# A third buffer for the attention output rows and two order edges on VectorE, with the mask and the dummy operand moved into idle buffers

## The chip, the cores and the metric

The kernel runs on one core of one Trainium2 chip. Its time is the device time of one execution in microseconds (us). It is the span that the profile shows, first to last instruction, plus 1.8 us. The profile also gives the mean clock that TensorE was granted: 1.0 is full speed.

## The reference

```python
h  = x + attention(layernorm(x)) @ wo        # x: 2048 tokens x 1024, bf16
h2 = h + mlp(layernorm(h))                   # gated MLP, hidden width 3584

phi = lambda t: where(t > 0, t + 1, exp(t)) + 1e-6
kv  = einsum("bhsd,bhse->bhde", phi(k), v)   # 32 heads of 32, linear attention
num = einsum("bhqd,bhde->bhqe", phi(q), kv)
o   = num / (einsum("bhqd,bhd->bhq", phi(q), sum_s phi(k)) + 1e-6)
```

## The kernel before

Three stages follow one another. Up to about 122 us, K and V are made and summed into `kv`. From there to about 290 us, the rows of the attention output are made, one row for each tile of 128 tokens, and the MLP's first products are fitted in between. From 290 us on, the MLP alone keeps TensorE busy. The change acts on the first two stages. I number the rows in the order in which they are made, from 0.

One row passes through these steps. Note the tags: a tag is a set of buffers that its tiles use in turn.

```python
def nd():                                      # the row's products and its division
    o_sb = bwork.tile([P, D], BF16, tag="o_sb", name="o_sb")      # bufs=2 from the pool
    for c0, n in pieces:                       # three pieces
        ps = ndpool.tile([P, NW], FP32, tag="ab", name="nd")      # one of three shared PSUM banks
        ...                                    # matmuls nd <- pqT, kvz
        nc.scalar.activation(out=den, ..., func=ACT.Ln)           # reciprocal on ScalarE
        nc.scalar.activation(out=rd, ..., func=ACT.Exp, scale=-1.0)
        nc.vector.tensor_tensor(out=ov[:, c0:c0 + n], in0=ndv, in1=rd, op=ALU.mult)
def oT():                                      # transpose of the row, a DMA from the SP queue
    nc.sync.dma_start_transpose(out=st["oT"], in_=st["o"][:])
def wo_h(borrow):                              # projection (attn), 2 x 8 matmuls, residual, normalization
    for j in range(2):
        if borrow: ps = pspool.tile(..., tag="E", bufs=2, name="attn")    # rows 6 to 9
        else:      ps = abpool.tile(..., tag="ab", name="attn")           # the same three banks as nd
        for c in range(KC):
            nc.tensor.matmul(ps[:], lhsT=st["oT"][:, c, :], rhs=wo_sb[:, c, ...], ...)
        added[t, j] = nc.vector.scalar_tensor_tensor(...)         # residual sum, frees the bank
    ...                                        # hn: two passes of ScalarE over the row
def hn_T():                                    # transpose of the normalized row, a DMA
    nc.sync.dma_start_transpose(out=hnT[s][i][:, :, r:r + P], in_=st["hn"][:])
```

The sums for the weights of the fast (Strassen) products are made by VectorE. Those of the query weights:

```python
def sums():
    nc.vector.tensor_tensor(out=t1, in0=b12, in1=b11, op=ALU.subtract)
    nc.vector.tensor_tensor(out=t2, in0=b22, in1=t1, op=ALU.subtract)     # "second sum"
    nc.vector.tensor_tensor(out=t3, in0=b22, in1=b12, op=ALU.subtract)    # "third sum"
    nc.vector.tensor_tensor(out=t4, in0=b21, in1=t2, op=ALU.subtract)
```

A scheduler decides, when the program is built, in which order each engine gets its instructions. It works from the program's dependences and buffers. This order then stays fixed: an engine that has come to an instruction waits there until its inputs are ready. The order of a built program can be read without running it.

## Time and profile before

| | before |
|---|---|
| median of its first three runs | 737.68 us (737.57 to 738.51) |
| span of the profiled execution | 737.2 us (its time, 739.0 us, is above that median) |
| TensorE busy | 722.7 us, 98% |
| longest waits of TensorE after the start | 0.8, 0.5, 0.5, 0.5 us |

The prediction shows the page and the waits. A line of the waits reads: engine, tile and source line that waited, the engine, tile and line waited for, then total us, times, longest us. A line of the timeline reads: start us, duration us, engine, source line, operation, out<-in, shape, count, and in brackets the idle time ahead of it with what ended it. `SPq` is the queue from which the DMAs are issued; its row is the issuing, not the moving of the data.

### The profile page before, as it was taken

To read this page: it belongs to the slowest core of one execution; us is meant where nothing else is said; L and a number is where in the kernel's file an instruction comes from. 1 tells how busy PE (TensorE), PEld (TensorE's weight loads), DVE (VectorE), ACT (ScalarE), POOL (GpSimd) and SP (SyncE) were. 2 spreads that over 40 slices of the span, in tenths; PEclk is the share of its full clock that TensorE was granted. 3 is DMA by queue.
4 is the path that set the end of the run, shared out by engine and by line. 5 is a ranking of instruction groups with operands and counts; after the bars stand their busy time and mean duration, and the time that the engine had idled before them with its cause. 6 is when DMAs were issued, how large, how long until landed. Compare 5 with 4: busy or idle time off the path is not lost.

```text
span 737.2 us, 10549 instructions
## 1 busy us (share of the span) xinstructions
PE 722.7 (98%) x3967; PEld 381.8 (52%) x4020; DVE 556.0 (75%) x980; ACT 321.5 (44%) x580; POOL 20.7 (3%) x56
## 2 busy tenths in 40 slices
PE   8999999999989999999999999999999999999997
PEld 3444555444444444444444444444444458888667
DVE  6997644676789767688768787887786479996677
ACT  4776553778786655444344444443444120000000
POOL 0000000000000000000000000000000001100210
PEclk9999999999999999999999999999999999999999
DMA  9765002079977526175638358575483499978932
GB/s 315 169 145 157 0 1 95 21 168 230 215 166 166 135 73 208 43 207 135 196 106 243 114 188 270 182 219 193 162 280 120 137 392 343 305 253 283 257 44 58
DMA packets 143811, 128.88 MB, mean 175 GB/s; under 512 B 50960, under 2 KB 126096, under 8 KB 143760
## 3 DMA queue, kind: packets, MB, share of 16 engines
q1 hardware_dynamic: 136688, 123.30, 55.6%
q0 software_dynamic: 5312, 3.15, 3.4%
q10 hardware_dynamic: 1760, 1.77, 0.7%
q8 instruction: 31, 0.51, 0.3%
q14 instruction: 20, 0.16, 0.1%
HBM read 76.81 MB, written 39.85 MB: 158 GB/s over the span
## 4 chain that ended last, share of the span: by engine, by line
PE 85%; DVE 7%; DMA 4%; ACT 3%; issue 1%; SPq 0%; DVEq 0%; POOL 0%; ACTq 0%
PE accA L832 22%; PE accX L832 8%; PE accY L832 8%; PE accA L1167 8%; PE attn L557 6%; PE Aq L733 4%; PE Aq L314 3%; PE accA L993 3%; PE accX L1167 3%; PE Aq L454 3%; PE accY L1167 2%; PE Eq L314 2%; PE accY L993 2%; PE accX L993 2%; PE Eq L733 2%; DVE stats L272 1%
## 5 line engine op out<-in xcount | busy, mean ns | idle before, releaser
L842 ACT ACTIVATE gu<-gu 128x512 bf16<-128x512 bf16 x72 | 45.4, 630 | 131.3 <-DVE gu L841 131.3
L837 ACT COPY snap<-accA 128x1024 f32<-128x1024 f32 x72 | 72.5, 1008 | 36.5 <-PE accA L832 36.4
L832 PEld LDWEIGHTS <-tg 128*128 128x128 f16 x384 | 37.6, 98 | 45.3
L832 PEld LDWEIGHTS <-tu 128*128 128x128 f16 x384 | 37.6, 98 | 45.3
L557 PE MATMUL attn<-wo_mem,oT 128*128 128x512 bf16 x247 | 57.9, 379 | 2.6 <-DVE o_sb L534 1.3
L841 DVE TENSOR_TENSOR gu<-accY,snap 128x1024 bf16<-128x1024 f32 x36 | 43.9, 1219 | 10.0 <-ACT snap L837 10.0
L832 PE MATMUL accA<-hn,tg 128*128 128x512 f16 (+1 forms) x192 | 49.3, 379 | 0.0
L832 PE MATMUL accA<-hn,tu 128*128 128x512 f16 (+1 forms) x192 | 49.3, 379 | 0.0
L841 DVE TENSOR_TENSOR gu<-accX,snap 128x1024 bf16<-128x1024 f32 x36 | 43.9, 1219 | 6.4 <-PE accX L832 3.7
L154 ACT COPY u<-Aq 128x512 f32<-128x512 f32 x54 | 31.3, 581 | 36.6 <-PE Aq L314 19.3
L1167 PEld LDWEIGHTS <-x 128*128 128x128 f16 (+1 forms) x448 | 43.9, 98 | 5.5
L832 PEld LDWEIGHTS <-wu 128*128 128x128 bf16 x288 | 28.2, 98 | 34.0
L832 PEld LDWEIGHTS <-wg 128*128 128x128 bf16 x288 | 28.2, 98 | 34.0
L557 PEld LDWEIGHTS <-oT 128*128 128x128 bf16 x256 | 24.6, 98 | 32.5 <-issue 4.1
L845 DVE TENSOR_TENSOR hq<-gu 128x512 bf16<-128x512 bf16 x48 | 20.3, 423 | 14.3 <-ACT gu L842 14.2
L314 PEld LDWEIGHTS <-xT 128*128 128x128 bf16 (+1 forms) x192 | 18.6, 98 | 23.6 <-issue 2.3
L534 DVE TENSOR_TENSOR o_sb<-nd,rd 128x384 bf16<-128x384 f32 (+1 forms) x48 | 23.4, 508 | 8.3 <-ACT rd L533 6.1
L1131 POOL DMA_DIRECT2D out_dram<-o x12 | 15.2, 1265 | 508.8 <-DMA h<-h_dram 419.1
L1167 PEld LDWEIGHTS <-xs 128*128 128x128 f16 x280 | 27.4, 98 | 3.2
L560 DVE SCALAR_TENSOR_TENSOR x_res<-attn,x_res 128x512 bf16<-128x512 f32 x32 | 22.0, 686 | 8.6 <-PE attn L557 8.5
L1173 DVE TENSOR_TENSOR snap<-accA,u 128x1024 f32<-128x1024 f32 x16 | 19.5, 1221 | 11.4 <-PE accA L1167 11.3
L993 PEld LDWEIGHTS <-x 128*128 128x128 bf16 (+1 forms) x168 | 16.4, 98 | 19.6
(235 smaller groups left out, 1420.3 us busy)
## 6 DMA issues: line engine op xcount, KB each, us to landing
x<-x_dram SPq DMA_DIRECT2D x17, 896.0 KB, 8.8
x_dram<-hq SPq DMA_DIRECT2D x28, 512.0 KB, 3.2
wg<-in_B_W_gate_dram SPq DMA_DIRECT2D x14, 512.0 KB, 5.1
wu<-in_B_W_up_dram SPq DMA_DIRECT2D x14, 512.0 KB, 7.3
wraw<-in_B_W_down_dram SPq DMA_DIRECT2D x14, 512.0 KB, 4.9
x_dram<-hq SPq DMA_DIRECT2D x28, 256.0 KB, 2.7
t_dram<-wt SPq DMA_DIRECT2D x28, 256.0 KB, 2.2
xd<-x_dram SPq DMA_DIRECT2D x6, 896.0 KB, 6.9
```

The source lines that it names most:

```text
L154: copies[nm, v] = nc.scalar.copy(out=snaps[nm, v], in_=bank[v][:])
L314: nc.tensor.matmul(ps[:], lhsT=left[m - 1][:, kc, r + v * P:r + (v + 1) * P], rhs=right[m - 1][:, kc, :], start=(start and kc == 0), stop= ...
L454: nc.tensor.matmul(ps[:], lhsT=rq[m - 1][:, kc, (c + v) * P:(c + v + 1) * P], rhs=left[m - 1][:, kc, :], start=(start and kc == 0), stop=( ...
L534: nc.vector.tensor_tensor(out=ov[:, c0:c0 + n], in0=ndv[:, :, 0:P].rearrange("p k (h e) -> p k h e", h=HPC), in1=rd[:, 0:n, :].unsqueeze(3 ...
L557: nc.tensor.matmul(ps[:], lhsT=st["oT"][:, c, :], rhs=wo_sb[:, c, j * NW:(j + 1) * NW], start=(c == 0), stop=(c == KC - 1))
L733: nc.tensor.matmul(ps[:], lhsT=w(v, m)[:, kc, :], rhs=left[m - 1][:, kc, :], start=(start and kc == 0), stop=(kc == KH - 1), skip_group_ch ...
L832: nc.tensor.matmul(ps[:, v, :], lhsT=w[v][n - 1][:, kc, :], rhs=left[n - 1][:, kc, :], start=(t is not None and kc == 0), stop=(kc == KH - ...
L837: nc.scalar.copy(out=st[nm][:], in_=halves(st["A"]))
L841: add(out=g[:], in0=halves(st[nm]), in1=st[base][:], op=ALU.add)
L842: nc.scalar.activation(out=g[:, 0, :], in_=g[:, 0, :], func=ACT.Relu)
L993: nc.tensor.matmul(ps[:, t * NW:(t + 1) * NW], lhsT=x_tile(n, s, kh)[:, f, (t0 + t) * P:(t0 + t + 1) * P], rhs=w_tile(n, kh)[:, f, :], sta ...
L1167: nc.tensor.matmul(pv[:, tt, :], lhsT=left(m)[:, f, tt * P:(tt + 1) * P], rhs=right(m)[:, f, :], start=(t is not None and f == 0 and tt % ...
```

## The change

It has three parts. The first edge holds the second sum of the query weights behind the first elementwise piece of the last K unit. The second holds the clip of the last Q unit's exponential behind the ninth token tile's residual sum. And `o_sb` gets three buffers in place of two. To pay for the third, the mask moves into a buffer of the tag "hn" and the operand of the start's dummy products into `kvz`.

```diff
+    def behind(late, first):
+        tc.add_manual_dep(late.ins, first.ins.name, ...NoSync..., reason="order")
 ...
-        q_sums()
+        behind(q_sums(), k_begins[NU - 1, 0, 0, 0])              # first edge; q_sums returns the second sum
+        mask = bwork.tile([P, D], BF16, tag="hn", bufs=HB, name="mask")[:, 0:NDW]
 ...
-            zero = asmall.tile([P, NW], BF16, tag="zero", bufs=1, name="zero")
+            zero = kvz[:].rearrange("p c w -> p (c w)")[:, 0:NW]
 ...
-            o_sb = bwork.tile([P, D], BF16, tag="o_sb", name="o_sb")
+            o_sb = bwork.tile([P, D], BF16, tag="o_sb", bufs=3, name="o_sb")
 ...
+    behind(q_ends[NS - 1, KH - 2, 1, 0], added[order[STS], 0])   # second edge
```

Left out of the print: the returns that hand the named instructions on, two small statistics tiles that become one, and `bufs=3` in two other places with the same tag. An edge of this kind makes no wait. It only tells the scheduler which of two instructions of one engine comes first.

More of the change, by code (lines that the diff above doesn't have):

```diff
@@ L61, in block_kernel @@
     make_identity(nc, ident[:])
-    mask = consts.tile([P, NDW], FP32, name="mask")
-    nc.gpsimd.memset(mask[:], 0.0)
-    for hh in range(HPC):
-        nc.gpsimd.memset(mask[hh * Dh:(hh + 1) * Dh, hh * Dh:(hh + 1) * Dh], 1.0)
-        nc.gpsimd.memset(mask[hh * Dh:(hh + 1) * Dh, P + hh:P + hh + 1], 1.0)
     deps = consts.tile([P, 1], FP32, name="deps")
@@ L133, in sums @@
             nc.vector.tensor_tensor(out=t1, in0=b12, in1=b11, op=ALU.subtract)
-            nc.vector.tensor_tensor(out=t2, in0=b22, in1=t1, op=ALU.subtract)
+            second = nc.vector.tensor_tensor(out=t2, in0=b22, in1=t1, op=ALU.subtract)
             nc.vector.tensor_tensor(out=t3, in0=b22, in1=b12, op=ALU.subtract)
             nc.vector.tensor_tensor(out=t4, in0=b21, in1=t2, op=ALU.subtract)
+            return second
         return (b11, b21, b22, t4, t1, t2, t3), sums
@@ L208, in phi_begin @@
         if m is None:
-            nc.scalar.activation(out=dst, in_=ps[:], func=ACT.Identity, bias=negb[:, 1:2], scale=1.0)
-        else:
-            nc.vector.scalar_tensor_tensor(out=dst, in0=ps[:], scalar=1.0 + PHI_EPS, in1=m,
-                                           op0=ALU.add, op1=ALU.add)
+            return nc.scalar.activation(out=dst, in_=ps[:], func=ACT.Identity, bias=negb[:, 1:2], scale=1.0)
+        return nc.vector.scalar_tensor_tensor(out=dst, in0=ps[:], scalar=1.0 + PHI_EPS, in1=m,
+                                              op0=ALU.add, op1=ALU.add)
     def phi_end(dst, e):
         nc.scalar.activation(out=e, in_=dst, func=ACT.Exp, bias=negb[:, 0:1], scale=1.0)
-        nc.vector.tensor_scalar(out=e, in0=e, scalar1=1.0, scalar2=PHI_EPS, op0=ALU.min, op1=ALU.add)
+        clipped = nc.vector.tensor_scalar(out=e, in0=e, scalar1=1.0, scalar2=PHI_EPS, op0=ALU.min, op1=ALU.add)
         nc.vector.tensor_tensor(out=dst, in0=dst, in1=e, op=ALU.max)
+        return clipped
+    def behind(late, first):
+        tc.add_manual_dep(late.ins, first.ins.name,
+                          mybir.DependencyInfo(mybir.DependencyClass.NoSync, mybir.DependencyReason.DATA),
+                          reason="order")
+    normed, k_copies, k_begins, q_ends = {}, {}, {}, {}
     order = [(i * HS + s * SW) // P + tt for s in range(NS) for i in range(2) for tt in range(NT)]
@@ L272, in ln_T @@
                 nc.vector.bn_stats(out=stats[:, k, :], in_=x_sb[:, k * NW:(k + 1) * NW])
-            mv = asmall.tile([P, nc.vector.BN_AGGR_DIM], FP32, tag="mv", name="mv")
-            nc.vector.bn_aggr(out=mv[:], in_=stats[:])
-            sm = asmall.tile([P, 3], FP32, tag="sma", name="sma")
-            lnv, rstd, nmr = (sm[:, k:k + 1] for k in range(3))
+            mv = asmall.tile([P, nc.vector.BN_AGGR_DIM + 3], FP32, tag="mv", name="mv")
+            nc.vector.bn_aggr(out=mv[:, 0:nc.vector.BN_AGGR_DIM], in_=stats[:])
+            lnv, rstd, nmr = (mv[:, nc.vector.BN_AGGR_DIM + k:nc.vector.BN_AGGR_DIM + k + 1] for k in range(3))
             nc.scalar.activation(out=lnv, in_=mv[:, 1:2], func=ACT.Ln, bias=LN_EPS, scale=1.0)
@@ L287, in ln_T @@
             nc.vector.scalar_tensor_tensor(out=nmr, in0=mv[:, 0:1], scalar=-1.0, in1=rstd, op0=ALU.mult, op1=ALU.mult)
-            nc.scalar.activation(out=xn[:], in_=x_sb[:], func=ACT.Identity, bias=nmr, scale=rstd)
+            normed[t] = nc.scalar.activation(out=xn[:], in_=x_sb[:], func=ACT.Identity, bias=nmr, scale=rstd)
             if t not in atiles[:PE_T]:
@@ L305, in block_kernel, with token_unit @@
         pk, vs = {}, {}
-        def token_unit(u, right, fin):
+        def token_unit(u, right, fin, copies={}):
             s, _, r = place(units[u][0])
@@ L316, in mm @@
                                      stop=(kc == KH - 1), skip_group_check=True)
-            return strassen(pspool, awork, mm, fin)
+            return strassen(pspool, awork, mm, fin, 3, False, copies)
         def new_pk(t):
@@ L330, in fin @@
                     new_pk(t)
-                phi_begin(pk[t][:, j * NW:(j + 1) * NW], ps, m)
+                k_begins[u, i, j, v] = phi_begin(pk[t][:, j * NW:(j + 1) * NW], ps, m)
                 ready[t] = ready.get(t, 0) + 1
                 if ready[t] == 2:
-                    e = bwork.tile([P, D], BF16, tag="o_sb", name="e")
+                    e = bwork.tile([P, D], BF16, tag="o_sb", bufs=3, name="e")
                     phi_end(pk[t], e[:])
-            return token_unit(u, rk, fin)
+            return token_unit(u, rk, fin, k_copies.setdefault(u, {}))
         def k_plain(t):
@@ L341, in k_plain @@
             new_pk(t)
-            e = bwork.tile([P, D], BF16, tag="o_sb", name="e")
+            e = bwork.tile([P, D], BF16, tag="o_sb", bufs=3, name="e")
             for j in range(2):
@@ L395, in block_kernel @@
         with tc.high_priority():
-            zero = asmall.tile([P, NW], BF16, tag="zero", bufs=1, name="zero")
-            nc.vector.memset(zero[:], 0.0)
+            zero = kvz[:].rearrange("p c w -> p (c w)")[:, 0:NW]
+            nc.vector.memset(zero, 0.0)
             spin = pspool.tile([P, NW], FP32, tag="A", bufs=2, name="spin")
             for n in range(SPIN):
-                nc.tensor.matmul(spin[:], lhsT=zero[:, 0:P], rhs=zero[:], start=True, stop=True)
+                nc.tensor.matmul(spin[:], lhsT=zero[:, 0:P], rhs=zero, start=True, stop=True)
             ln_T(atiles[0])
@@ L432, in block_kernel @@
         rq, q_sums = right_ops(wq_sb, tq)
-        q_sums()
+        behind(q_sums(), k_begins[NU - 1, 0, 0, 0])
+        mask = bwork.tile([P, D], BF16, tag="hn", bufs=HB, name="mask")[:, 0:NDW]
+        nc.gpsimd.memset(mask, 0.0)
+        for hh in range(HPC):
+            nc.gpsimd.memset(mask[hh * Dh:(hh + 1) * Dh, hh * Dh:(hh + 1) * Dh], 1.0)
+            nc.gpsimd.memset(mask[hh * Dh:(hh + 1) * Dh, P + hh:P + hh + 1], 1.0)
         for t in units[-1]:
@@ L439, in block_kernel @@
             nc.vector.tensor_tensor(out=kvz[:, c, :], in0=kv_ps[bnk][:, i * NDW:(i + 1) * NDW],
-                                    in1=mask[:], op=ALU.mult)
+                                    in1=mask, op=ALU.mult)
     abctx = ExitStack()
@@ L462, in fin @@
                 e = qw[-1].tile([P, 2, NW], BF16, tag="e", name="e")
-                phi_end(pair, e[:])
+                q_ends[s, c, i, j] = phi_end(pair, e[:])
         return strassen(pspool, qw[-1], mm, fin, 3, s == NS - 1 and c + 2 == KH)
@@ L790, in block_kernel @@
     for t, copy in ((order[-2], ("m1", 1)), (order[-1], ("u3", 1))):
-        tc.add_manual_dep(squared[t].ins, quad_copies[2][copy].ins.name,
-                          mybir.DependencyInfo(mybir.DependencyClass.NoSync, mybir.DependencyReason.DATA),
-                          reason="order")
+        behind(squared[t], quad_copies[2][copy])
     pqctx.close()
```

## The prediction

> **What bounds the kernel now.** I read the page's busy line and slices first, then the waits of the tensor engine, then the timeline around each wait that the change touches.
>
> ```profile
> span 737.2 us, 10549 instructions
> PE 722.7 (98%) x3967; PEld 381.8 (52%) x4020; DVE 556.0 (75%) x980; ACT 321.5 (44%) x580; POOL 20.7 (3%) x56
> PE   8999999999989999999999999999999999999997
> DVE  6997644676789767688768787887786479996677
> PEclk9999999999999999999999999999999999999999
> ```
>
> TensorE (PE) is busy in 98% of the span, at full clock, in every slice but the first and the last. All time in which no matmul runs is 737.2 - 722.7 = 14.5 us. In the trace, 1.2 and 1.7 us of that lie at the start (before the first dummy matmul, and before the first input tile is normalised) and 3.7 us after the last matmul, which ends at 733.5. The change touches none of these 6.6 us, so at most 14.5 - 6.6 = 7.9 us are within reach of any reordering in the middle. From 290 us on (the MLP) the matmuls stand one behind the other with no wait listed against them, so a microsecond won before 290 should arrive at the end undiminished.
>
> Which waits make up the 7.9 us is in the view of who waited for whom, for PE (total us, times, longest):
>
> ```profile
> PE attn L557 <- DVE o_sb L534: 1.3, 4, 0.5
> PE attn L557 <- DVE x_res L560: 0.8, 1, 0.8
> PE nd L527 <- DVE o_sb L534: 0.5, 1, 0.5
> PE Dq L314 <- DVE wo_mem L211: 0.5, 1, 0.5
> ```
>
> Each is a wait for VectorE to read a PSUM bank and so free it. The rest is start-up waits, two waits for ScalarE and one for weight sums, 0.2 to 0.5 us each, and sequencer delays. The four lines are 3.1 us together; the change is aimed at them.
>
> **What the Trainium skill says.** (1) "PSUM — Partial Sum Buffer", section "Engine vs sequencer instructions": the VectorE queue is strict FIFO. The trace agrees: below, an instruction whose input is ready stands 1.7 us behind one that waits for ScalarE. So the order in which the scheduler places VectorE work can cost PE time even where VectorE has idle time. (2) "Perfetto Trace Analysis", section "Optimization Strategy": consistent bubbles on the engine that should be saturated can mean that there is no room for the next tile. Here that points to a third row buffer, but the trace shows only one clear such wait, not a repeating one. (3) The same page, section "DMA Instruction — HWDGE (DVE, Sync)": the row of a DMA instruction does not hold the data's movement. The trace agrees: the row transposes are rows of 1.24 us in the median, but land 3.4 us after issue, and a row buffer is free only then. (4) "VectorE: DVE Perf Modes", section "The perf-mode tier table": a tensor_tensor with a PSUM operand runs at 1x. So a bf16 mask instead of fp32 should not quicken the masking (8 of 284 ns, 128x132). Comparing with the 128x512 PSUM instructions of 690 ns, the slope is (690 - 284)/(512 - 132) = 1.07 ns per column, which is about one element a cycle at the page's 0.96 GHz.
>
> **First edge** (the second sum for Wq behind the first phi of the last K unit). Timeline, start and duration:
>
> ```profile
> 69.03 1.03 PE L314 MATMUL Dq<-pq_mem,xT 128*128 128x512 bf16 x4
> 70.39 1.22 DVE L134 TENSOR_TENSOR tq<-wq_sb,tq 128x2048 f16<-128x2048 bf16 x1
> 71.52 0.68 DVE L211 SCALAR_TENSOR_TENSOR wo_mem<-Dq,m 128x512 bf16<-128x512 f32 x1
> 72.26 1.02 PE L314 MATMUL Dq<-pq_mem,xT 128*128 128x512 bf16 x4 [0.47 <-DVE wo_mem L211]
> ```
>
> The Dq bank is full at 70.06, but VectorE takes L134 first, and L211 starts 1.13 us later than it could. The Dq tag has one bank, so the second Dq waits. With L211 at 70.39 the bank is free at 71.07, before PE needs it (71.6). Gain: the 0.47 us wait plus some issue delay, about 0.5 us, if nothing else takes L134's place. The third sum (L135, 1.22 us) needs only the first, not the second, and has no edge. If the scheduler puts it there, nothing is won. I count 60%: 0.3 us.
>
> **Second edge** (the clip of the last Q unit's exponential behind the residual add of the ninth token tile).
>
> ```profile
> 207.59 3.61 PE L557 MATMUL attn<-wo_mem,oT 128*128 128x512 bf16 x15
> 210.93 0.43 DVE L217 TENSOR_SCALAR e<-e 128x1024 bf16<-128x1024 bf16 x1 [0.94 <-ACT e L216]
> 211.28 0.69 DVE L560 SCALAR_TENSOR_TENSOR x_res<-attn,x_res 128x512 bf16<-128x512 f32 x1
> 212.02 0.59 PE L557 MATMUL attn<-wo_mem,oT 128*128 128x512 bf16 x2 [0.82 <-DVE x_res L560]
> 213.09 0.34 PE L527 MATMUL nd<-kvz,pq_mem 128*128 128x132 bf16 x3 [0.48 <-DVE o_sb L534]
> 219.50 1.04 PE L733 MATMUL Aq<-hs,tg 128*128 128x512 f16 x4 [0.41 <-DVE tg L644]
> ```
>
> The first half of the projection is eight matmuls of 0.216 us from 207.59, with a tail to some 209.5. VectorE is done with its earlier work at 209.99, then idles 0.94 us in front of L217, with L560 ready behind it. With the edge L560 runs in that hole. Both PE waits, 0.82 + 0.48 = 1.30 us, can shrink to near nothing. But after 211 VectorE works without a hole until the sums for the first weight tile (L644), for which PE waits at 219.50. All of that moves up only by what VectorE wins: one L560 out of the line, 0.60 us start to start. PE then arrives early and waits longer there. So I count 0.65 us, not 1.30.
>
> **Three row buffers.**
>
> ```profile
> 152.66 1.23 SPq L541 DMA_TRANSPOSE oT<-o_sb  x1
> 155.92 1.02 DVE L534 TENSOR_TENSOR o_sb<-nd,rd 128x384 bf16<-128x384 f32 x2 [1.35 <-PE Aq L454]
> 156.53 3.61 PE L557 MATMUL attn<-wo_mem,oT 128*128 128x512 bf16 x15 [0.51 <-DVE o_sb L534]
> ```
>
> The third row is written at 155.92, though its reciprocals were done at 154.12 and 154.52. The transpose out of the buffer that it takes was issued at 152.66 and landed at 155.80 (landing events of the trace), which is what released it; the view names a matmul that had long ended. Three PSUM banks serve both these products and the projection, so PE waits 0.51 us for the third row. A third buffer removes this: 0.5 us. The fourth row (written 161.26, transpose of its buffer landed 161.14, reciprocals 161.05) can win up to 0.15 us. For later rows, the transpose has landed before the reciprocal is done, and the write waits for ScalarE or stands in VectorE's queue, so a third buffer buys nothing. In the K stage the same tag holds the exponentials; the view of that tile lists 0.7 us of ScalarE waits, and none of PE that comes from them. I count 0.55 us.
>
> **What pays for it.** Nine GpSimd memsets of the mask, 88 to 213 ns, some 1.25 us overlapped, move from 0.9 to 2.1 us to somewhere before 122, when the masking starts. GpSimd is 3% busy: no cost. The dummy operand in kvz is still one VectorE memset. Two statistics tiles become one: no instruction more or less. The bf16 mask: no change, as above.
>
> **Sum.** 0.3 + 0.65 + 0.55 = 1.5 us. Earlier VectorE work around 156 and 211 should relieve a few of the 0.1 to 0.2 us waits behind it: 0.3 us. 737.7 - 1.8 gives **735.9 us**, a fast run.
>
> **Rivals.** (a) Another instruction fills the hole: the third Wq sum at 70.4, or another VectorE row in front of L560. For it: the scheduler put L134 there because it was ready, and L135 is as ready. Against: each edge names just one instruction, which looks like a hole examined. It leaves 736.5 to 737.7. (b) The order is shuffled: with the row buffer free sooner, the products of the next row are placed earlier and take one of the three shared PSUM banks from the projection. For: all bank waits are on these three. Against: ScalarE's reciprocals, often over 1 us behind the products, mostly set the row's pace, not its buffer. It could give back 1 to 2 us: 736.5 to 738.5. (c) The mask takes its slot of the two "hn" buffers early, while the K stage still normalises its input there. One buffer would then cycle per tile through a 1.24 us write and a 3.5 us transpose, some 5 us against the 2.5 to 3.5 us that the tiles now have between 24 and 42 us, and PE would starve by several us: 742 or more. Against: residual loads that share a tag with the input loads start in the trace only after the last of these (41.63 against 39.68), so order within a tag seems to be kept. 3%. (d) All waits named go, VectorE's too, by a kinder order after 211: 0.5 + 1.3 + 1.2 us and follow-ups, 734.
>
> **Range and chances.** The sum and rival (d) set the low end, rivals (a) and (b) the high end: 734.2 to 738.0. Faster by 2% would need 14.8 us, more than all of PE's idle time: 0.5%. Slower by 2% needs rival (c) in full: 1%.
>
> **What would show it.** PE's wait for L211 near 72 gone, with L211 before L134 and L135; L560 in front of the clip near 210 and the PE waits of 0.82 and 0.48 gone, with a longer wait for the weight sums near 218; the third row written near 154.5 and the wait near 156.5 gone; PE busy time unchanged and the span less by the lost waits; the masking still at once after the last kv product. I am wrong if new PE waits for PSUM banks appear between 150 and 260, if the input stage before 65 us is stretched, or if the gain is already lost again when the MLP starts near 290.

## More of the kernel before

From the timeline of the kernel before, the transpose of row 6 and the projection that stands after it:

```profile
185.89 1.29 SPq L541 DMA_TRANSPOSE oT<-o_sb  x1
190.14 4.26 PE L557 MATMUL attn<-wo_mem,oT 128*128 128x512 bf16 x18
```

The first three of these eighteen products are row 6's, the others row 5's (from the order of the built program; the record of one product of row 5 is missing). The transpose landed at 189.50, by its landing events in the trace, and TensorE took the first product at 190.14, with no wait listed. Row 6 was there 0.64 us ahead of time.

## The result

| | before | after |
|---|---|---|
| median of 6 runs | 738.26 us (737.57 to 739.62) | 743.44 us (741.80 to 743.70) |
| ratio | | 1.0065 [1.0051, 1.0078] |
| mean clock of the executions | | 0.997 in four, 0.999 in two |

Ratios are the mean time of one kernel's runs over that of the other's of the same rounds, so they are not quite the ratio of the medians; in brackets stands the 95% interval. A mean clock of 0.997 over a span of 740 us is a stretch of a few microseconds at half speed. The change made the kernel slower by about 5 us, 0.65%. That is "the same" within 2%, but above the predicted range of 734.2 to 738.0.

From the page of the kernel after:

```profile
span 741.9 us, 10603 instructions
PE 727.6 (98%) x4020; PEld 382.1 (51%) x4020; DVE 556.8 (75%) x980; ACT 321.0 (43%) x580; POOL 20.8 (3%) x56
PEclk9999999999999999999999999999999999999999
```

Two traps lie here. TensorE looks busier by 4.9 us, but the trace of before has 53 matmul records fewer (3967 against 4020) for as many products, so busy times of TensorE can't be compared this closely. And the clock row shows nothing, because a slice is 18.5 us long and its digit means "90% or more". The waits of TensorE tell more:

```profile
PE attn L564 <- DMA oT<-o_sb: 3.2, 1, 3.2
PE attn L564 <- DVE o_sb L541: 1.4, 3, 0.5
```

The first is new: one wait of 3.2 us, for the transpose of a row. In the timeline (L588 transposes a normalized row, L548 an attention row, L581 is the normalization's first pass):

```profile
185.26 1.45 SPq L588 DMA_TRANSPOSE hn<-hn  x1
188.24 2.94 SPq L548 DMA_TRANSPOSE oT<-o_sb  x1
191.26 1.15 ACT L581 ACTIVATE hn<-x_res,sm 128x1024 bf16<-128x1024 bf16 x1 [3.13 <-DMA hn<-hn]
194.10 6.18 PE L564 MATMUL attn<-wo_mem,oT 128*128 128x512 bf16 x20 [3.17 <-DMA oT<-o_sb]
```

TensorE stands in front of row 6. By the built order, twelve of row 6's matmuls now stand ahead of row 5's sixteen, though row 5's transpose had landed at 185.99. The table of stretches, of 2 us each, then shows what follows (from, to, length, busy us with count of PE, PEld, DVE, ACT, POOL, then the clock, DMA share, GB/s):

```profile
194.00:196.00 2.00, 1.90 (x7) 0.74 (x8) 1.52 (x4) 1.97 (x7) 0.18 (x1) 0.71 0.86 230
196.00:198.00 2.00, 2.00 (x6) 0.70 (x5) 0.53 (x2) 0.00 (x0) 0.00 (x0) 0.50 0.62 178
```

After the stand the clock is at half for 3.4 us: only six matmuls lie in the 2 us from 196 on, against eleven at full clock (shown further below). "TensorE: Matmul & The Clock Gate", section "What's actually happening", of the Trainium skill says that TensorE falls to half clock after an idle window of about 3.4 us, one of a free-running series 3413 ns long, and comes back after about as long a busy one. The trace agrees on the length, since its record of the half clock is 3413 ns long, and every whole stretch of its clock record is a multiple of that (55, 1 and 159 times).

So the windows can be counted back from the record. No window had to be idle in full: the half clock began at 194.84, TensorE was at work again from 194.10, and so it had been idle for 2.7 us of the 3.4 us window before. Nor need it be one wait: in row_order_late_load (below) two waits of 1.47 and 1.08 us in one window were enough. In the 16 traces the half clock followed on each of the four windows before 700 us with 2.1 to 2.7 us of idle time, and on none with 1.7 us or less (the start of the kernel left out). The wait of 2.17 us of fetch_earlier_12, which two windows shared, was not followed by it.

The sum: 190.56 to 194.10 is 3.54 us from one matmul's start to the next, less the usual 0.22 makes 3.3 us. The 28 matmuls from 194.10 on took 7.74 us up to the next product (201.84). At full clock they take 28 x 0.216 = 6.05, so the half clock cost 1.7 us. Together that is 5.0 us. The spans differ by 4.7. Two further readings agree. The two executions of the kernel after whose mean clock was 0.999 took 741.80 and 742.51 us, on average 1.4 us less than the four with 0.997. And counted by TensorE's weight loads (the n-th of one trace against the n-th of the other), the kernel after is 0.3 us ahead of the kernel before at 190 us, 5.1 us behind at 200, and 4.5 behind at 290 and at 700: the loss arises in this one place and arrives at the end.

### The profile page after: what moved, and what is told of

Read it like the earlier page. It is cut to its first block, busy times and chain, and to the rows that moved or that the text cites. A ratio compares the mean times of both kernels' runs of the same rounds, so it can differ in the third digit from the quotient of the medians.

```text
span 741.9 us, 10603 instructions
## 1 busy us (share of the span) xinstructions
PE 727.6 (98%) x4020; PEld 382.1 (51%) x4020; DVE 556.8 (75%) x980; ACT 321.0 (43%) x580; POOL 20.8 (3%) x56
## 4 chain that ended last, share of the span: by engine, by line
PE 83%; DVE 7%; ACT 4%; DMA 4%; issue 1%; SPq 0%; POOL 0%; DVEq 0%; POOLq 0%
PE accA L838 22%; PE accX L838 8%; PE accY L838 8%; PE accA L1173 8%; PE attn L564 6%; PE Aq L740 4%; PE accA L999 3%; PE Aq L316 3%; PE accX L1173 3%; PE Aq L461 2%; PE accY L1173 2%; PE Eq L316 2%; PE accY L999 2%; PE accX L999 2%; PE Eq L740 2%; DVE stats L275 1%
## 5 line engine op out<-in xcount | busy, mean ns | idle before, releaser
L564 PE MATMUL attn<-wo_mem,oT 128*128 128x512 bf16 x256 | 60.3, 387 | 4.7 <-DMA oT<-o_sb 3.2
```

## The experiments

All kernels gave correct results. The kernel before ran beside each group on the same chip: 738.12 us in the first, 738.68 in the second, 738.05 in the third, 738.72 in the fourth. Some of these executions had a stretch at half clock too (0.997: 739.72 and 740.11), which is the scatter to keep in mind.

### Which part did it

**edges_two_buffers.** The whole change, with `bufs=3` taken out.

```diff
-            o_sb = bwork.tile([P, D], BF16, tag="o_sb", bufs=3, name="o_sb")
+            o_sb = bwork.tile([P, D], BF16, tag="o_sb", name="o_sb")
```

> The changed kernel with the attention rows back at two buffers; both edges and all moved storage kept. Theory ORDER (the third buffer makes the scheduler put twelve matmuls of row 6's projection in front of row 5's, and row 6's transpose then lands 3.2 us late, after which TensorE runs 3.4 us at half clock): with two buffers only three matmuls of row 6 stand in front of row 5, as before, so no wait over 1 us between 180 and 200, clock 1.000, and the time is 0 to 1.5 us under before (ratio 0.998 to 1.000), some 5 to 6 us under the changed kernel. Rival EDGES OR STORAGE (the edges, or the mask, dummy operand and merged statistics tile cause the loss): still 742 to 744 us.

Measured: 740.25 us, ratio 1.0027 [1.0012, 1.0042]. The wait of 3 us is gone, but the kernel is 2 us slower than before, not up to 1.5 us faster as expected. In the timeline of 216 to 220 us:

```profile
216.53 0.42 DVE L112 TENSOR_TENSOR hs<-hn 128x512 f16<-128x512 bf16 x1 [1.84 <-DMA hn<-hn]
217.48 0.34 PE L534 MATMUL nd<-kvz,pq_mem 128*128 128x132 bf16 x3 [1.68 <-DVE o_sb L541]
219.88 0.82 PE L740 MATMUL Eq<-hs,tg 128*128 128x512 f16 x3 [1.09 <-DVE tg L647]
```

TensorE waits 1.68 us for the row and 1.09 us for the weight sums. The order of the built program differs from before in this place on TensorE as well, so this run alone does not say whether the edge or the order that came with it cost the time.

**buffers_no_edges.** The whole change without either edge.

```diff
-        behind(q_sums(), k_begins[NU - 1, 0, 0, 0])
+        q_sums()
-    behind(q_ends[NS - 1, KH - 2, 1, 0], added[order[STS], 0])
```

> The changed kernel without both edges; three row buffers and all moved storage kept. In the built program TensorE, ScalarE and the DMA queue have the very order of the changed kernel, only VectorE differs, by the second and third sum for Wq. ORDER: the same wait of about 3.2 us for row 6's transpose and the half-clock stretch, 742 to 744 us, and the wait for the first phi near 72 us stays at 0.3 to 0.5 us with or without the edge. Rival EDGES: back to 737 to 739 us.

Measured: 743.52 us, ratio 1.0071 [1.0054, 1.0088], clock 0.997 in all four executions; the wait in front of row 6 is 3.02 us. So the edges are not the cause of the loss. The built programs also showed that, with three buffers, taking the second edge out alters no engine's order at all: there it does nothing. The first edge does nothing visible either. With the edge, the kernel after waits 0.30 us near 72 us; without it, this one waits 0.20 us:

```profile
72.02 1.02 PE L316 MATMUL Dq<-pq_mem,xT 128*128 128x512 bf16 x4 [0.20 <-DVE wo_mem L206]
```

**storage_only.** Both edits above together: two buffers and no edge, so that only the moved mask and dummy operand are left.

> What is left of the change when both edges and the third row buffer are taken out: only the mask and the dummy operand in other tiles, and the small statistics joined. Built, its order on every engine is that of the kernel before except for the place of the memsets. Theory (the moved storage is free; the loss of the kernel with two edges and two buffers belongs to its second edge): within 0.5 us of the kernel before, ratio 0.9993 to 1.0007. Rival (the moved storage itself costs the 2 us that the kernel with two edges and two buffers lost): 739.5 to 741, and long waits of TensorE for the row and the exponential weight sums in the last third, 1.5 us and over.

Measured: 739.69 us (737.87 to 740.60), ratio 1.0006 [0.9994, 1.0018]. The scatter was wide; its executions at 0.997 and 0.998 are 739.69 and 740.60. Its ratio can't be told from 1, and none of the long waits is there (the longest after the start is 0.8 us, at the place of the first edge). Within what the interval leaves (0.4 us won to 1.3 us lost), payment was free, as predicted.

**second_edge_held.** Two buffers, and the second edge as nothing but a swap of two neighbours on VectorE. The order of every engine was fixed, instruction by instruction, to that of storage_only, apart from this swap:

```diff
+    for chain in HELD.values():                # per engine: the wanted order, by instruction number
+        for first, late in zip(chain, chain[1:]):
+            behind(MADE[f"I-{late}"], MADE[f"I-{first}"])
```

The built program was compared with the wanted one: two positions on VectorE differ and nothing else. (A helper records the instructions here, so all lines below carry one line number.)

> Moved storage, two row buffers, and the second edge as one swap: on VectorE the residual sum stands ahead of the clipping of the exponential, and nothing else is moved on any engine. The kernel with both edges and two buffers was 2 us slower, with other orders on TensorE and ScalarE too. Theory (there the order that follows cost, not the swap): within 0.5 us of the moved storage alone, that is 737.6 to 739.0; my prediction of the swap's gain was 0.65 us. Rival (the swap itself costs, as it holds the clipping and with it the next row): waits of TensorE for the row at 211 to 220 grow by 1 us and more, 739.5 to 740.5.

Measured: 738.93 us (738.62 to 739.24), ratio 1.0008 [0.9995, 1.0022]. It neither gains the 0.65 us that I had counted nor clearly loses against the kernel before; against storage_only, which ran in another group, 0.65 us can't be resolved. The timeline shows what became of the gain:

```profile
209.37 0.69 DVE L31 SCALAR_TENSOR_TENSOR x_res<-attn,x_res 128x512 bf16<-128x512 f32 x1
210.21 0.43 DVE L31 TENSOR_SCALAR e<-e 128x1024 bf16<-128x1024 bf16 x1
217.57 0.42 DVE L31 TENSOR_TENSOR hs<-hn 128x512 f16<-128x512 bf16 x1 [1.15 <-DMA hn<-hn]
218.04 1.02 PE L31 MATMUL Eq<-hs,tg 128*128 128x512 f16 x4 [1.03 <-DVE hs L31]
```

The swap is there, the residual sum ahead of the clip, and TensorE's wait for that sum is not listed. (It is 0.82 us in the profile before, 0.38 in storage_only and not listed in held_order, which both lack the swap, so its size belongs to the execution as much as to the order.) But VectorE then stands 1.15 us before the sums of the normalized row, whose transpose lands at 217.54, and TensorE stands 1.03 us behind it. In the kernel before that transpose landed at 217.46 and VectorE came to it at 217.55. In storage_only, whose order is held here, VectorE already waits 0.20 us for it. The swap does not move its issue (212.14 there, 212.30 here), so there was no room to come earlier; its longer flight here, 5.24 against 4.78 us, adds to the wait. As to the open question of edges_two_buffers, most of its 2 us seems to belong to the order that came with the edges and not to the swap, but the two intervals overlap, so this is not shown.

**mended_edge_two_buffers.** Two buffers, no second edge, and the first edge on the third sum as well.

```diff
-        behind(q_sums(), k_begins[NU - 1, 0, 0, 0])
+        for late in q_sums():                   # second and third sum
+            behind(late, k_begins[NU - 1, 0, 0, 0])
```

> Two row buffers, no second edge, and the first edge laid on both the second and the third sum of the query weights, so that neither can fill the hole ahead of the first elementwise piece of the last key unit. Theory (the third sum was what kept the first edge from paying): TensorE's wait at the first query product for VectorE is 0.1 us or nothing instead of 0.30, and the time is 0.3 to 0.6 us under that of the kernel with moved storage alone. Rival (the piece waits for its own bank and not for a sum): wait and time as with storage alone, within 0.2 us.

Measured: 737.95 us (737.56 to 741.05), ratio 0.9997 [0.9982, 1.0012] to before. The mechanism is as expected: the elementwise piece comes to stand ahead of both sums, starts at 70.93, and the product that waited for it follows unhindered (no bracket):

```profile
71.67 1.02 PE L316 MATMUL Dq<-pq_mem,xT 128*128 128x512 bf16 x4
```

The size is not resolved. One of its six executions fell into a stretch at half clock (741.05), and the other five lie between 737.56 and 738.46.

### The buffer or the order

**row_order.** The whole change, with row 6's first products held behind row 5's last.

```diff
+    for j in range(2):
+        behind(products[order[6], j, 0], products[order[5], 1, KC - 1])
```

> The changed kernel, plus an order edge on TensorE alone: row 6's projection behind row 5's last matmul. ORDER: row 5's transpose has landed 8 us before, so the 3.2 us wait near 191 and the half-clock stretch go; minus 5 us against the changed kernel, 737.5 to 739 us in these units, about as before. If the losses lie elsewhere (rival LAYOUT: somewhat slower everywhere), it stays at 742 or more, with the wait gone.

Measured: 740.87 us, ratio 1.0035 [1.0020, 1.0050], clock 0.999 to 1.0. The stand and the half clock are gone, yet only 2.2 (by the ratios) to 2.6 (by the medians) of some 5 us come back, which neither forecast had. The scheduler also moved other instructions of every engine but GpSimd. Row 5 now waits in turn:

```profile
190.99 1.15 ACT L581 ACTIVATE hn<-x_res,sm 128x1024 bf16<-128x1024 bf16 x1 [2.88 <-DMA hn<-hn]
194.75 3.61 PE L564 MATMUL attn<-wo_mem,oT 128*128 128x512 bf16 x16 [1.18 <-DVE o_sb L541]
```

Its bank is one of the three that the rows share, and is held by row 7's products until VectorE has read them. VectorE waits for the reciprocals, and these stand on ScalarE behind a pass that waited 2.88 us for a buffer whose transpose was slow. Another wait of 1.0 us came at 213.

**held_order.** Three buffers, no edges, and the order of every engine held to that of storage_only (by the same loop as above; built: no difference on any engine). Only where the rows lie is changed.

> Moved storage and three row buffers, no edges, and the order of every engine held, instruction by instruction, to that of the kernel with moved storage and two buffers (built: no difference on any engine). Only where the rows of the attention output lie is changed. Theory (the third buffer is harmless and the order that it let through is the loss): no wait of TensorE over 1.3 us past the start, no half clock after one, row 2 written from 154.4 on in place of 155.9, and a time of 737.4 to 738.6, between the prediction's gain of 0.55 us and nothing. Rival (the third buffer costs by itself, for instance through transposes that now meet): 740 to 743.5, as with the order left free.

Measured: 737.34 us (736.88 to 738.02), ratio 0.9989 [0.9976, 1.0001]. Against buffers_no_edges, from which it differs in the order alone, it is 6 us faster (0.9989 against 1.0071). From its timeline, in order: row 2's write, row 0's projection, row 6's transpose, and the projection of rows 6 and 5:

```profile
154.60 1.01 DVE L32 TENSOR_TENSOR o_sb<-nd,rd 128x384 bf16<-128x384 f32 x2
155.99 2.32 PE L32 MATMUL attn<-wo_mem,oT 128*128 128x512 bf16 x10
185.19 1.23 SPq L32 DMA_TRANSPOSE oT<-o_sb  x1
189.44 4.26 PE L32 MATMUL attn<-wo_mem,oT 128*128 128x512 bf16 x19
```

Row 2 is written at 154.60 in place of 155.92, and the projection starts at 155.99 with no wait listed, in place of 156.53 after 0.51 (storage_only, with the same order and two buffers, has 155.94, 156.56 and 0.51): this is the gain of the buffer as I had worked it out. The transpose of row 6 lands 3.05 us after issue and TensorE takes it 1.20 us later without a wait. So the third buffer does no harm. The order that the scheduler made from it does.

**held_order_mended.** The same, with the mended first edge, held to the order of mended_edge_two_buffers.

> As the held order with three buffers, and with the first edge on both the second and the third sum, the whole order held to that of the two-buffer kernel with that mended edge (built: no difference on any engine). If the mended edge's 0.5 to 0.7 us (wait at the first query product) and the third buffer's 0.0 to 0.6 us add up, it is 737.0 to 738.0 and the fastest of all. Rival (either is taken back at the next wait): as the held order alone, within 0.2 us.

Measured: 737.51 us (736.68 to 738.62), ratio 0.9991 [0.9978, 1.0003]. Its times are not below those of held_order; one execution with a clock of 0.998 is among them. Both are the fastest. Against the kernel after they win some 5.5 us by the ratios. Against the kernel before, the intervals just reach 1, so a gain of about 0.1% is likely and not shown.

### Why row 6 is late

Rows 5 and 6 stood in an odd order in the kernel before too (three of row 6's products ahead of row 5), without harm, because row 6 was there. This is row 6 in three traces, in us:

| | written | transpose issued | landed | flight |
|---|---|---|---|---|
| before | 185.81 | 185.89 | 189.50 | 3.61 |
| after | 187.13 | 188.24 | 194.06 | 5.82 |
| held_order | 185.11 | 185.19 | 188.24 | 3.05 |

Of the 4.56 us by which it lands later, 1.32 is the later write, 1.03 the later issue (a weight load and a store stand ahead of it in the queue), and 2.21 the longer flight. My first explanation of the flight was the 512 KB weight load issued at 186.80.

**load_behind_transpose.** The whole change, with that load held behind row 6's transpose in the queue.

```diff
+    behind(weights[6], turned[order[6]])
```

> The changed kernel, plus an order edge on the DMA queue: the weight load of step 6 behind row 6's transpose, instead of in front of it. The built order then has all sixteen matmuls of row 6 in front of row 5, directly behind row 7's products, so overtaking is stronger than in the changed kernel. Rival FLIGHT (overtaking is harmless by itself; the loss is that the transpose is issued 1 us late and flies 5.8 us beside a weight load instead of 3.1 to 3.6): the transpose flies 3.1 to 3.6 us and the wait for it falls to under 1 us, 738 to 740 us. ORDER in its strict form (overtaking alone costs, whatever the load does): a wait of 2 to 4 us stays, 742 or more.

Measured: 742.77 us (740.96 to 744.88), ratio 1.0062 [1.0035, 1.0089]. In the profiled execution (740.96) the transpose was issued at 187.37, landed after 4.36 us and TensorE waited 1.53 us; no half clock followed. Two of the four executions had clocks of 0.997 and 0.995 and took 744.3 and 744.9. Neither forecast was met, and the run does not isolate the load: its own issue moved only to 189.84, so it still ran beside the last 1.9 us of the flight, and with the edge all sixteen of row 6's products came to stand ahead of row 5's.

**row_order_late_load.** Row order as above, and the load issued one step later.

```diff
-            for _ in range(-(-len(early_loads) // (QSTEPS - step))):
+            for _ in range(0 if step == 6 else -(-len(early_loads) // (QSTEPS - step))):
```

> The whole change, with row 5's products ordered ahead of row 6's and the weight load of step 6 issued one step later. With the order alone (740.87) TensorE still waited about 1.3 us extra for row 5, as row 7's reciprocals stood behind a normalized row whose transpose took 5.9 us beside that load. Theory (what is left of the loss is that transpose's flight beside the load): the transpose lands in 3.0 to 3.8 us, the wait of row 5 falls to 0.5 us or less, and the time is 738.5 to 739.8. Rival (three row buffers cost in other places, for instance the wait of 1.2 us at the products at 212): 740.3 to 741.3, as with the order alone.

Measured: 743.20 us, ratio 1.0055 [1.0042, 1.0068]. A miss. The normalized row's transpose took 5.69 us with no weight load in flight, row 6's took 4.53 us, row 5 waited 1.21 us as with the row order alone, and two more waits (1.47 and 1.08 us, at 212 to 215) were followed by half clock. The load is not what made this transpose slow.

What the DMA view of 185 to 191.5 us showed instead was one packet of 16 KB of kind "instruction" in the middle of that flight, and after it some 1.3 us in which hardly any bytes moved. The same kind of packet lies at 187.8 us in the kernel after. "Runtime: NRT & Kernel Launch", section "Instruction fetch mechanics", of the Trainium skill says that the engines' programs are fetched in blocks of 16 KB, of 256 instructions, while the engine runs. There are 31 such packets in the trace, which agrees: TensorE's 4020 weight loads and 4020 products make 31.4 blocks of 256.

**fetch_earlier_24 and fetch_earlier_12.** The whole change, with tiny products at the start, in TensorE's waiting time, so that the 16 KB blocks end at other places of the program. All else keeps its order.

```diff
+            for n in range(26):                 # 14 in the other; two of the sixteen dummies are left out
+                nc.tensor.matmul(spin[:, 0:32], lhsT=zero[:, 0:P], rhs=zero[:, 0:32], start=True, stop=True)
```

> The whole change, with 26 tiny products (32 columns) in place of two of the sixteen dummy products at the start, while TensorE waits there for its first input: 24 products more in all, order of everything else as in the whole change. The instruction fetches of TensorE come at every 128th product or so, so the one at 187.8 us should come 24 products, some 5 us, earlier, near 182.6, before the transpose of the normalized row (issued 185.3) and that of row 6 (188.2), but still beside the same weight load. Theory (the fetch is what made both slow): the normalized row's transpose lands in 3.0 to 4.6 us instead of 5.9, row 6's in 3.0 to 4.6 instead of 5.8, TensorE's wait for row 6 falls from 3.17 to 0.3 to 1.6 us, no half clock follows, and the time is 738.5 to 741.5. Rival (the weight load is what made them slow): flights of 5.5 to 6.0 us, wait 3 us, half clock, 743 to 744.

> As the other, with 12 products more in all: the fetch comes some 2.6 us earlier, near 185.2, just as the normalized row's transpose is issued and 3 us ahead of row 6's. Theory (the fetch): the normalized row's transpose is still slow, 5 us or more, and row 6's takes 3.0 to 4.6 us; TensorE's wait for row 6 is 0.5 to 2 us and no half clock follows in most executions; 739.5 to 742. Rival (the load): no change, 743 to 744.

Measured: 745.81 us, ratio 1.0095 [1.0078, 1.0111], and 745.94 us, ratio 1.0097 [1.0080, 1.0114]. Both missed. The fetch did move ahead of the two transposes in fetch_earlier_24, though to 185.9 and not to 182.6.

```profile
187.98 1.45 SPq L29 DMA_TRANSPOSE hn<-hn  x1
191.45 2.23 SPq L29 DMA_TRANSPOSE oT<-o_sb  x1
196.46 4.02 PE L29 MATMUL attn<-wo_mem,oT 128*128 128x512 bf16 x9 [3.58 <-DMA oT<-o_sb]
```

Still the first took 5.52 us and the second 4.96, now beside the load alone. In fetch_earlier_12 the fetch lay in the first flight only: 4.91 and 4.18 us, a wait of 2.17 us and no half clock. Both kernels lost about 1 us more near 72 us: in fetch_earlier_12 a fetch had been moved beside the transpose of an input tile, VectorE waited 0.84 us for it, and TensorE 1.16 us behind VectorE. So neither the load nor the fetch is the single cause: with one of them taken away, the first flight stayed as long. Over the 16 profiled executions, the transposes issued between 140 and 275 us divide as follows. A load counts as beside a flight when the two, from issue to landing, overlap at all, and a packet when its own time does.

| beside the flight | transposes | median flight, us |
|---|---|---|
| neither | 255 | 3.28 |
| a 512 KB weight load | 154 | 3.80 |
| a 16 KB instruction packet | 42 | 4.32 |
| both | 45 | 5.35 |

This is a count over traces and not an experiment. What in the DMA engines lengthens the flight stays open.

### The half clock

**warm_filler.** The whole change, with twelve useless products ahead of row 6's.

```diff
+                if t == order[6] and j == 0:
+                    for n in range(12):
+                        nc.tensor.matmul(ps[:], lhsT=wo_sb[:, 0, 0:P], rhs=wo_sb[:, 0, 0:NW], start=True, stop=True)
```

> The whole change, with twelve products of no use (2.6 us at 0.216 us each) put into row 6's bank just ahead of its own products, which overwrite it. TensorE stands still in front of row 6 for 0.5 us at most instead of 3.17. Theory (the loss is two things, the stall for row 6's transpose and the half clock that follows from standing still): no stretch of half clock in any execution, mean granted clock 0.999 or 1.0, time 741 to 742, that is 1.5 to 2.5 us under the whole change; the stall itself is still paid, by the useless products. Rival (the half clock is due to something else, not to standing still): clock 0.997 again and the stretch of 3.4 us still there, time 743 to 744.5.

Measured: 746.37 us, ratio 1.0102 [1.0088, 1.0116]. A miss. The half clock behind row 6 was gone in the profile, but the time was 3 us over the whole change. The scheduler had made another order around the new products, so the run tells nothing more.

**filler_held.** The same with the order held; built, the twelve products are the only difference to the kernel after.

> The whole change with twelve useless products ahead of row 6's, and this time the order of every engine held to that of the whole change, so that the useless products (2.6 us at 0.216 us each) are all that differs; the first such try lost its time elsewhere, as its order had changed. Theory (standing still for 3.2 us is what takes the clock down, and costs some 2 us after the wait): TensorE waits 0.4 to 0.9 us for row 6, no half clock between 194 and 200, clock 0.999 or 1.0, and 741.2 to 742.4, that is 1.1 to 2.2 us under the whole change. Rival (the half clock is not due to the standing still): clock 0.997, a stretch at half clock near 196 as before, 743 to 744.

Measured: 744.02 us (742.95 to 744.91), ratio 1.0078 [1.0066, 1.0091], clock 0.999 to 1.0 in all five executions.

```profile
193.78 6.22 PE L32 MATMUL attn<-wo_mem,oT 128*128 128x512 bf16 x28 [0.31 <-DMA oT<-o_sb]
196.00:198.00 2.00, 2.00 (x11) 0.93 (x10) 0.18 (x1) 0.00 (x0) 0.00 (x0) 1.00 0.73 202
```

The wait is 0.31 us, eleven matmuls begin between 196 and 198, and by 225 us TensorE is 2.0 us ahead of the kernel after (224.63 against 226.64 for the same row's first product). So the standing still is what took the clock down there. The expected time was still missed, because the lead was lost later: 1.0 us at 267, where a normalized row's transpose took 4.53 us with an instruction packet beside it, against 3.05 us in the kernel after, and the rest in small waits up to 610 us that I did not follow.

## Why the prediction was wrong

**The bound.** Right: TensorE is the bound, and every difference found above is a wait of TensorE or its clock. But "at most 7.9 us are within reach" counts only what can be won. What can be lost has no such limit, and the page of the kernel before can't show it. And the 7.9 us were too many, since the 14.5 us of idle time also held the missing records: gaps of under 0.15 us sum to 3.5 us in that trace and to 0.6 in that of held_order, where no record is missing. (One slice in the middle, 203 to 221 us, also stood at 8 and not at 9.)

**First edge.** The risk named there came true: the third sum took the place of the second.

```profile
70.32 1.22 DVE L130 TENSOR_TENSOR wq_sb<-wq_sb 128x2048 f16<-128x2048 bf16 x1
71.45 0.68 DVE L206 SCALAR_TENSOR_TENSOR wo_mem<-Dq,m 128x512 bf16<-128x512 f32 x1
72.19 1.02 PE L316 MATMUL Dq<-pq_mem,xT 128*128 128x512 bf16 x4 [0.30 <-DVE wo_mem L206]
```

The wait is 0.30 us in place of 0.47, and not even this is the edge's work, since buffers_no_edges has 0.20 without it and edges_two_buffers 0.54 with it. With both sums behind the piece, it was gone.

**Second edge.** With three buffers it had nothing to do. With two, the wait that I named was not listed, but the 0.65 us were not there. Wrong here is "All of that moves up only by what VectorE wins": the sums in that line wait for a transposed row that lands at 217.5, so nothing moves up.

**Three row buffers.** The mechanism of the step is right where the order is held: row 2 written at 154.60 (I had said near 154.5) and the wait of 0.51 us gone. In the kernel after, the row is written on time as well, but little is won, because the new order puts only two of five products ahead of row 0's projection, and TensorE waits in front of it for nearly as long as before:

```profile
154.41 1.34 DVE L541 TENSOR_TENSOR o_sb<-nd,rd 128x384 bf16<-128x384 f32 x3
155.79 1.90 PE L564 MATMUL attn<-wo_mem,oT 128*128 128x512 bf16 x8 [0.49 <-DVE o_sb L541]
```

The view names VectorE, which was done at 155.75; row 0's transpose landed at 155.75 too (155.89 in held_order, where five products filled the time), so this projection could not have come sooner.

**What pays for it.** Right: storage_only can't be told from before, and the masking was not late; its interval leaves room for a loss of up to 1.3 us.

**The step that failed** is the dismissal of rival (b), "The order is shuffled". I took a row's pace to be set by ScalarE's reciprocals and gave a new order "1 to 2 us", with 738.5 as its end. The runs showed the new order to be the whole loss: the same three buffers without edges take 743.5 us with the order left free (1.0071) and 737.3 with the old one (0.9989). The size was off because I had looked for lost PSUM banks only, and the new wait was for a DMA. The shuffle also moved the DMA queue, which put row 6's transpose 2.35 us later and into a stretch where its flight took 2.21 us more, for a reason that stays open. TensorE's fixed order turned that into 3.3 us of standing, and the half clock added 1.7 us. Rival (c), the mask in the way of the K stage, did not happen.

## What to carry to other kernels

A buffer more, or an edge, is an input to the scheduler: compare the built order on every engine, the DMA queue too, before believing a local gain, and if the order has changed, test the buffer with the old order held. Look for places where a fixed order relies on a transfer that lands only just in time; here 0.64 us of room became a loss of 5 us. Idle time of TensorE that adds up to more than 2 us within one window of 3.4 us can cost more than its length, since here the half clock followed (1.7 us more).

## What the Trainium skill lacked or had wrong

- "TensorE: Matmul & The Clock Gate" speaks of an idle window of about 3.4 us before the half clock, and of gaps above about 3 us, in its closing table, or above about 3.4 us. Here windows with 2.1 to 2.7 us of idle time in 3.4 us were followed by the half clock, once made up of two waits of 1.47 and 1.08 us. A wait of 3.0 to 3.2 us (in the two profiled executions) was followed by 3413 ns of it in eight of ten executions (four of six of the whole change, four of four of buffers_no_edges, judged by the mean clock of 0.997), at a cost of 1.7 us in the one that was worked out.
- "Runtime: NRT & Kernel Launch" calls the cost of a fetch of 16 KB of instructions mostly hidden. No listed wait of TensorE in the kernel after is put down to it, but row transposes with such a fetch beside them took 4.32 us in the median against 3.28 without, and 5.35 if a weight load was there too (a count, no experiment).
- I found no page that gives the flight of a DMA transpose beside other transfers, or that says that a buffer count can change the order of instructions on other engines; the runs show 3.05 to 5.82 us for one and the same row's transpose, and 6 us for the order.
